# Global contexts in 96-row chunks, the global pieces of a step beside its local contexts, score copies on ScalarE

## The chip, the core and the metric

The kernel runs on one core of a Trainium2 chip. The metric is the device time of one execution in microseconds. In this text PE is TensorE (matmuls and transposes), ACT is ScalarE, DVE is VectorE, POOL is GpSimd, and SP starts the DMAs. "mm" is one matmul instruction.

## What is computed

The reference is a windowed attention with 32 global positions, followed by two feed-forward blocks, all in float32:

```python
s_g = scale * q_g @ k_all.T                      # global queries see everything
out_g = sm(s_g) @ v_all
s_ll = where(|i - j| <= 32, scale * q_l @ k_l.T, -1e9)
s_lg = scale * q_l @ k_g.T
out_l = sm(concat(s_lg, s_ll)) @ concat(v_g, v_l)
x = concat(out_g, out_l)  ->  (2176 tokens used, 512)
h = max(x @ w1, x @ w2, x @ w3);  y = h @ w_out          # 512 -> 768 -> 512
out = softplus(y @ w2_in) @ w2_out                       # 512 -> 2048 -> 512
```

There are 4 batches, 8 heads of width 64, 512 local and 32 global positions. The weights arrive as 64-bit words and are decoded to float32 on the chip.

## The kernel before

**Attention.** The local work is cut into 32 groups `k` (batch, half of the 512 positions, pair of heads). A generator, `att_stream`, runs step `k`: `s1(k)` makes the masked scores of group k in PSUM (matmuls with 64 rows of contraction into 64 columns, the form 64\*64 in the profile) and lets DVE copy them out with their minimum (L154); `s1e` is the exponential on ACT (L161); `s1f` divides by the sum (DVE L167, POOL L171). `s2` transposes group k-2 on PE (L221, L222) and `s2e` copies the two transposed tiles `pwt` and `pgt` out of PSUM. `s3` multiplies group k-3 with the values (L248, L252, form 128\*64) and `s3h`, `s3l` copy the result out as a high and a low part.

**Global queries.** In every odd step `s1g` makes a part of the global scores (L187, L193, form 128\*64). After the fourth pair of a half, `gsoft` does their softmax, `g2` transposes them (L287, L290), `g2e` copies them into the tile `gt`, and in the next step `g3` multiplies them with the values: five chunks of 128, 128, 128, 64 and 96 rows, two heads each, for two pairs of heads (L311, 20 mm, which the trace shows as 40), and `g3e` copies that out.

**Feed forward, first block.** `up(u, f, i)` is one product set: 12 mm of 128\*128 for unit u (256 or 288 tokens), column block f and weight i (L540 to L542). `rest` takes the maximum of the three (ACT L551, DVE L554). `split_h` splits it into a high part `hh` (copy on ACT for u = 0, 1, 7 and on DVE otherwise, L569, L571) and a low part `hl` (L572). `down` is the product with `w_out` (L586 to L588). `dec_stream` decodes the 24 weights of the first block, four DVE instructions, two on ACT and one on POOL each.

**What sets the order.** Every engine runs its instructions in the order in which the program issues them. The program interleaves by counters: `step()` advances the attention by one `yield`, `more(x)` by x of them on average, and `fill`, `part(x)` advance the decoding. Steps below `KS` = 12 run first, with few product sets between them. Then all sets of units 0 and 1 follow with `FJ` = 2.3 yields of decoding each; from then on 1.35 (`RA`) attention yields follow each product set and 1.4 (`RD`) or 1.35 each down block. PSUM tiles of attention and products come from one pool, `pm`, of five buffers (`ptile`).

In steps from 12 on, the global pieces stand behind the fourth `yield` of the step, so product sets lie between them and the local pieces:

```python
for c in late:
    g3(*c)
if k < n and k % 2 == 1:
    s1g(k)
for c in late:
    g3e(*c)
```

The second block (lines from 1063 on) follows after the attention and is not touched.

Of the kernel before, what the change touches and what calls it, by code (L numbers as in the profile page):

```python
# [21 lines left out]
def body(ctx, tc, kq, vw, vb, qg, w1, w2, w3, w_out, w2_in, w2_out, out):  # L22
# [6 lines left out]
    KS = 12  # L29
    HHA = 2  # L30
    HLP = 6
    XLP = 0
    wp = ctx.enter_context(tc.tile_pool(name="wp", bufs=24, side="left"))
# [167 lines left out]
    def gsoft():  # L201
        t = gpend.pop(0)
        nm = at.tile([128, 1], F32, tag="gnm", name="gnm")
        sm = at.tile([128, 1], F32, tag="gsm", name="gsm")
        nc.vector.tensor_reduce(out=nm, in_=t, axis=mybir.AxisListType.X, op=ALU.min)
        yield 0
        nc.scalar.activation(t, t, AF.Exp, scale=-1.0, bias=nm, accum_out=sm)
        yield 0
        nc.vector.tensor_scalar(sm, sm, 1e-9, None, op0=ALU.add)
        nc.vector.reciprocal(sm, sm)  # L210
        nc.vector.tensor_scalar(t, t, sm, None, op0=ALU.mult)
        yield 0
# [12 lines left out]
    def s2e(k):  # L225
        g = st[k]
        pw, pg = g.pop("p")
        if k < KW:
            pwt = wp.tile([128, 512], F32, tag="w", name="pwt")
        else:  # L230
            pwt = at.tile([128, 512], F32, tag="pwt", name="pwt", bufs=1)
        pgt = at.tile([128, 128], F32, tag="pgt", name="pgt", bufs=3)
        nc.scalar.activation(pgt, pg, AF.Copy)  # L233
        if k >= KS or k % 2 == 0:
            nc.scalar.activation(pwt, pw, AF.Copy)
        else:
            nc.vector.tensor_copy(pwt, pw)
        g["pgt"], g["pwt"] = pgt, pwt
# [34 lines left out]
    def s3l(k):  # L273
        b, hf, pr = groups[k]
        po = st.pop(k)["po"].rearrange("p u n -> p (u n)")
        if (2 * b + hf, pr) in direct:
            xh, xl = xs[2 * b + hf]
            nc.vector.tensor_tensor(xl[:, pr:pr + 1, 0:256], po.unsqueeze(1), xh[:, pr:pr + 1, 0:256].bitcast(F32), op=ALU.subtract)

    def g2(b, s):  # L280
        c = gs[b, s]
        t = c["t"]
        chunks = [(0, 128), (128, 128), (256, 128), (384, 64), (448, 96)]
        pa = ptile([128, 512], "pa")
        pb = ptile([128, 128], "pb")
        gt = at.tile([128, 5, 128], F32, tag="gt", name="gt", bufs=1)
        nc.tensor.transpose(pb[0:96], t[:, 448:544], ident)  # L287
        for i in range(4):
            o, n = chunks[i]
            nc.tensor.transpose(pa[0:n, 128 * i:128 * i + 128], t[:, o:o + n], ident)  # L290
        c["gt"], c["p"] = gt, (pa, pb)
# [8 lines left out]
    def g3(b, s, joint=None):  # L300
        c = gs[b, s]
        gt, v0, v1 = c["gt"], c["v0"]["v"], c["v1"]["v"]
        vs = [(v0, 0, 128), (v0, 2, 128), (v1, 0, 128), (v1, 2, 64), (v1, 3, 96)]
        if joint is None:
            joint = ptile([128, 64], "pog")
        po = joint.rearrange("p (a n) -> p a n", n=32)
        for e in range(2):
            for j, (v, u, n) in enumerate(vs):
                for i in range(2):
                    h = 2 * e + i  # L310
                    nc.tensor.matmul(po[64 * i:64 * i + 64, e, :], lhsT=v[0:n, u, 64 * h:64 * h + 64], rhs=gt[0:n, j, 32 * h:32 * h + 32],  # L311
                                     start=(j == 0), stop=(j == 4), skip_group_check=True)
        c["po"] = po
# [11 lines left out]
    def att_stream():  # L325
        n = len(groups)
        load_kq(0)
        load_kq(1)
# [11 lines left out]
        yield 0  # L340
        late = []
        soft = iter(())
        p2 = p3 = um = ng = 0
        for k in range(n + 4):
# [4 lines left out]
            if k < KS:  # L349
# [12 lines left out]
                for c in late:  # L362
                    g3(*c, None if joint is None else joint[:, 288:352])
                if gq and q3 is not None:
                    s3h(q3)
                if gq and q2 is not None:
                    s2e(q2)
                s1e(k, 0)
                s1e(k, 1)
                if not (gq) and q3 is not None:  # L370
                    s3h(q3)
                if k:
                    s1f(k - 1)
                next(soft, None)
                if not (gq) and q2 is not None:
                    s2e(q2)
# [12 lines left out]
                for c in late:  # L389
                    g3e(*c)  # L390
                    ng += 1
                late = []
                if gq:
# [3 lines left out]
            else:  # L397
                if k == KS:
                    s1f(k - 1)
                if k < n:  # L400
                    s1(k, 0)
                    s1(k, 1)
                e3, e2 = (k - 3, k - 2) if k < n else (k - 2, n - 1)
                while p3 < p2 and p3 <= e3 or p2 <= e2:
                    if p3 < p2 and p3 <= e3:
                        s3(p3)
                        s3h(p3)
                        s3l(p3)
                        p3 += 1
                    if p2 <= e2:  # L410
                        s2(p2)
                        s2e(p2)
                        p2 += 1
# [6 lines left out]
                if k < n:  # L420
                    s1f(k)
                for c in late:
                    g3(*c)
                if k < n and k % 2 == 1:
                    s1g(k)
                for c in late:
                    g3e(*c)
                    ng += 1
                late = []
                next(soft, None)  # L430
# [131 lines left out]
    def split_h(u, f):  # L562
# [4 lines left out]
        m = ms.pop((u, f))  # L567
        if HHA > u or u == 7:
            nc.scalar.activation(hh, m, AF.Copy)  # L569
        else:  # L570
            nc.vector.tensor_copy(hh, m)  # L571
        (nc.gpsimd if u == 0 and f < HLP else nc.vector).tensor_tensor(hl, m, hh.bitcast(F32), op=ALU.subtract)  # L572

    def down(u, c, by_row=False):
# [3 lines left out]
        for f0, f1 in [(f, f + 1) for f in range(6)] if by_row else ((0, 5), (5, 6)):  # L578
            for j in range(2):
                p = ps[j]  # L580
                cs = slice(128 * (c + j), 128 * (c + j) + 128)
                for f in range(f0, f1):
# [4 lines left out]
                    nc.tensor.matmul(p, lhsT=w[:, 0, cs], rhs=hl, start=False, stop=False)  # L587
                    nc.tensor.matmul(p, lhsT=w[:, 1, cs], rhs=hh, start=False, stop=(f == 5))  # L588
        for j in range(2):
            o = hp.tile([128, 288], F32, tag="m", name="o")[:, 0:n]  # L590
# [234 lines left out]
    with tc.manual_schedule():  # L825
# [3 lines left out]
        cp = sp = pe = None  # L829
        FJ = 2.3  # L830
        AD = 3
# [3 lines left out]
        NS = 1  # L835
        D2L = 3.0
        D3L = 2.0
# [15 lines left out]
        RJ = 0.7  # L853
        RD = 1.4
        RA = 1.35
        au = [0]
# [8 lines left out]
        def more(x):  # L865
            nx[0] += x
            while nx[0] >= 1:
                nx[0] -= 1
                step()
# [24 lines left out]

        lag[0] = 3
        next(att)
# [14 lines left out]
        flush()  # L911
        lag[0] = 2
        while pos[1] < 18:
# [9 lines left out]
        for _ in range(AD):  # L923
            step()
            part(1.5)
        lag[0] = 0
# [27 lines left out]
        for u in range(6):  # L954
# [11 lines left out]
            for v, f, i in pairs_of(u):  # L966
                up(v, f, i)
                more(RA)
                wide(VU)
# [12 lines left out]
            for c in range(4):  # L982
# [4 lines left out]
                if u == 0:  # L987
                    fill(FD)
                more(RD if u < 2 else RA)
                wide(VD0)  # L990
                spill(SD)
            for _ in ldx:
                pass
            if u == 0:
                for f in range(6):
                    if f >= 1:
                        for _ in range(0):
                            step()
                    split_h(1, f)
                for _ in range(AS):  # L1000
                    step()
# [437 lines left out]
```

## Time and profile before

| | |
|---|---|
| time, median of 3 runs | 768.58 us (768.45 to 768.88) |
| profiled execution, its own time | 769.23 us |
| span of the profile | 767.5 us |
| PE busy | 749.8 us, 98% |
| DVE, ACT, POOL busy | 568.9, 371.9, 252.5 us |
| granted TensorE clock | 1.00 |

"Busy" is the time in which at least one instruction of an engine runs. Matmuls overlap in the pipeline, so on PE the distance from one start to the next says what an instruction costs, not its duration.

### The profile page before, as it was taken

To read this page: it belongs to the slowest core of one execution; us is meant where nothing else is said; L and a number is where in the kernel's file an instruction comes from. 1 tells how busy PE (TensorE), PEld (TensorE's weight loads), DVE (VectorE), ACT (ScalarE), POOL (GpSimd) and SP (SyncE) were. 2 spreads that over 40 slices of the span, in tenths; PEclk is the share of its full clock that TensorE was granted. 3 is DMA by queue.
4 is the path that set the end of the run, shared out by engine and by line. 5 is a ranking of instruction groups with operands and counts; after the bars stand their busy time and mean duration, and the time that the engine had idled before them with its cause. 6 is when DMAs were issued, how large, how long until landed. Compare 5 with 4: busy or idle time off the path is not lost.

```text
span 767.5 us, 18081 instructions
## 1 busy us (share of the span) xinstructions
PE 749.8 (98%) x6984; PEld 722.0 (94%) x6984; DVE 568.9 (74%) x1435; ACT 371.9 (48%) x950; POOL 252.5 (33%) x243
## 2 busy tenths in 40 slices
PE   6899999999999999999999999999999999999998
PEld 4689998999999999999999999999999999999998
DVE  6999956878776777785971656444686889999996
ACT  6875537655544643343322555434554344444443
POOL 4545532122111100443840688842981000000000
PEclk9999999999999999999999999999999999999999
DMA  9858107775867745776101554435549913444432
GB/s 338 317 205 327 41 38 239 238 257 200 278 206 233 239 139 193 275 256 220 43 1 56 184 197 142 175 144 179 183 151 387 374 49 111 138 137 138 139 97 83
DMA packets 78182, 141.03 MB, mean 184 GB/s; under 512 B 9360, under 2 KB 43280, under 8 KB 78096
## 3 DMA queue, kind: packets, MB, share of 16 engines
q1 hardware_dynamic: 78096, 139.88, 53.0%
q8 instruction: 55, 0.90, 0.5%
q14 instruction: 31, 0.25, 0.1%
HBM read 95.03 MB, written 44.83 MB: 182 GB/s over the span
## 4 chain that ended last, share of the span: by engine, by line
PE 77%; DVE 10%; ACT 4%; issue 3%; POOL 3%; DMA 2%; SPq 1%; DVEq 0%; POOLq 0%; ACTq 0%
PE pu L540 8%; PE pu L542 8%; PE pu L541 8%; PE z L1244 6%; PE z L1068 6%; PE z L1069 6%; PE z L1067 6%; PE z L1243 6%; PE z L1242 6%; PE ps L148 2%; PE pd L587 2%; PE pw L221 2%; PE po L248 2%; PE pd L588 2%; PE pd L586 2%
## 5 line engine op out<-in xcount | busy, mean ns | idle before, releaser
L540 PE MATMUL pu<-xh,w 128*128 128x256 f32 (+1 forms) x576 | 168.7, 293 | 0.4 <-ACT pgt L233 0.4
L541 PE MATMUL pu<-xl,w 128*128 128x256 f32 (+1 forms) x576 | 166.3, 289 | 0.0
L542 PE MATMUL pu<-xh,w 128*128 128x256 f32 (+1 forms) x576 | 166.0, 288 | 0.2 <-POOL w L477 0.2
L1244 PE MATMUL z<-v,oo 128*128 128x256 f32 x480 | 136.8, 285 | 0.5 <-DVE oo L1238 0.5
L1243 PE MATMUL z<-v,oo 128*128 128x256 f32 x480 | 135.5, 282 | 0.0
L1242 PE MATMUL z<-v,oo 128*128 128x256 f32 x480 | 135.2, 282 | 0.0
L1068 PE MATMUL z<-o,wi 128*128 128x272 f32 x448 | 129.1, 288 | 1.6 <-POOL o L673 1.6
L1069 PE MATMUL z<-o,wi 128*128 128x272 f32 x448 | 129.1, 288 | 0.0
L1067 PE MATMUL z<-o,wi 128*128 128x272 f32 x448 | 128.7, 287 | 0.1
L540 PEld LDWEIGHTS pu<-xh,w 128*128 128x128 f32 x576 | 108.7, 189 | 2.8 <-issue 1.2
L542 PEld LDWEIGHTS pu<-xh,w 128*128 128x128 f32 x576 | 108.3, 188 | 0.4 <-POOL w L477 0.4
L541 PEld LDWEIGHTS pu<-xl,w 128*128 128x128 f32 x576 | 108.6, 189 | 0.0
L1237 ACT ACTIVATE oo<-sm 128x640 fp32r<-128x640 f32 (+1 forms) x72 | 49.8, 692 | 93.7 <-DVE sm L1232 87.8
L1244 PEld LDWEIGHTS z<-v,oo 128*128 128x128 f32 x480 | 90.9, 189 | 1.4 <-DVE oo L1238 0.9
L1242 PEld LDWEIGHTS z<-v,oo 128*128 128x128 f32 x480 | 91.2, 190 | 0.1
L1243 PEld LDWEIGHTS z<-v,oo 128*128 128x128 f32 x480 | 90.9, 189 | 0.0
L1068 PEld LDWEIGHTS z<-o,wi 128*128 128x128 f32 x448 | 84.2, 188 | 2.3 <-POOL o L673 2.2
L171 POOL TENSOR_TENSOR s<-s,rs 128x512 f32<-128x512 f32 x32 | 35.3, 1103 | 151.0 <-DVE rs L168 85.0
L1067 PEld LDWEIGHTS z<-o,wi 128*128 128x128 f32 x448 | 84.5, 189 | 0.3 <-DVE h L1089 0.3
L1069 PEld LDWEIGHTS z<-o,wi 128*128 128x128 f32 x448 | 84.2, 188 | 0.0
L1238 DVE TENSOR_TENSOR oo<-sm,oo 128x640 fp32r<-128x640 f32 (+1 forms) x72 | 55.1, 765 | 16.5 <-ACT oo L1237 12.8
L673 POOL TENSOR_TENSOR o<-ot,o 128x544 fp32r<-128x544 f32 x36 | 50.9, 1426 | 45.8 <-DMA ot<-od 33.8
(165 smaller groups left out, 1642.1 us busy)
## 6 DMA issues: line engine op xcount, KB each, us to landing
gd<-a SPq DMA_DIRECT2D x32, 544.0 KB, 3.2
gl<-gd SPq DMA_DIRECT2D x32, 512.0 KB, 7.1
kq<-in_kq_dram SPq DMA_DIRECT2D x31, 368.0 KB, 5.1
raw<-in_w_out_dram SPq DMA_DIRECT2D x22, 512.0 KB, 4.5
raw<-in_w_dram SPq DMA_DIRECT2D x18, 512.0 KB, 6.5
vt<-in_vw_dram SPq DMA_DIRECT2D x16, 512.0 KB, 5.9
raw<-in_w_in_dram SPq DMA_DIRECT2D x16, 512.0 KB, 4.4
ot<-od SPq DMA_DIRECT2D x24, 272.0 KB, 3.2
```

Source lines behind the costliest of these rows:

```text
L540: nc.tensor.matmul(p, lhsT=w[:, 0, k], rhs=xh[:, k, 0:n], start=(k == 0), stop=False)
L541: nc.tensor.matmul(p, lhsT=w[:, 0, k], rhs=xl[:, k, 0:n], start=False, stop=False)
L542: nc.tensor.matmul(p, lhsT=w[:, 1, k], rhs=xh[:, k, 0:n], start=False, stop=(k == 3))
L673: nc.gpsimd.tensor_tensor(w[:, 1], src, w[:, 0].bitcast(F32), op=ALU.subtract)
L1067: nc.tensor.matmul(z, lhsT=w[:, 0, k], rhs=x[:, 0, k], start=st and k == 0, stop=False, skip_group_check=True)
L1068: nc.tensor.matmul(z, lhsT=w[:, 0, k], rhs=x[:, 1, k], start=False, stop=False, skip_group_check=True)
L1069: nc.tensor.matmul(z, lhsT=w[:, 1, k], rhs=x[:, 0, k], start=False, stop=sp and k == 1, skip_group_check=True)
L1237: nc.scalar.activation(oh[:, a:b], src, AF.Copy)
L1238: nc.vector.tensor_tensor(ol[:, a:b], src, oh[:, a:b].bitcast(F32), op=ALU.subtract)
L1242: nc.tensor.matmul(p, lhsT=oh[:, a], rhs=w[:, 0], start=st, stop=False, skip_group_check=True)
L1243: nc.tensor.matmul(p, lhsT=oh[:, a], rhs=w[:, 1], start=False, stop=False, skip_group_check=True)
L1244: nc.tensor.matmul(p, lhsT=ol[:, a], rhs=w[:, 0], start=False, stop=sp, skip_group_check=True)
```

## The change

Five things change; the amount of arithmetic on PE stays the same, instruction for instruction.

1. `gt` is allocated once, its rows 64 to 95 of chunk 3 are set to zero once, and the fourth chunk of `g3` contracts 96 rows instead of 64 (the added rows are zero on one side).
2. In steps from 12 on, `s1g`, `g3` and `g3e` are issued by `globals_of(k)` right behind `s3`, `s3h`, `s3l` of the step, `s1g` ahead of `g3`.
3. `pwt` is always copied by ACT (before: by DVE in odd steps below 12).
4. `hh` of unit 2 is copied by ACT.
5. The counters change: `FJ` 2.3 to 2.1, `D2L` (decoding yields per early step) 3.0 to 2.5; attention yields per product set 1.35, 1.35, 1.1, 1.3 for units 2 to 5; per down block 1.8 for unit 0, 1.3 for unit 1 and 1.4 beyond.

All other new names are off (0) and issue nothing.

```diff
-    HHA = 2
+    HHA = 3
...
-        if k >= KS or k % 2 == 0:
+        if not PWD >> k & 1:
             nc.scalar.activation(pwt, pw, AF.Copy)
         else:
             nc.vector.tensor_copy(pwt, pw)
...
-        gt = at.tile([128, 5, 128], F32, tag="gt", name="gt", bufs=1)
+        gt = gts[0]
...
-        vs = [(v0, 0, 128), (v0, 2, 128), (v1, 0, 128), (v1, 2, 64), (v1, 3, 96)]
+        vs = [(v0, 0, 128), (v0, 2, 128), (v1, 0, 128), (v1, 2, 96), (v1, 3, 96)]
...
+        gts.append(at.tile([128, 5, 128], F32, tag="gt", name="gt", bufs=1))
+        nc.vector.memset(gts[0][64:96, 3, :], 0.0)
...
+        def globals_of(k):
+            nonlocal ng
+            if todo[0] is None:
+                return
+            todo[0] = None
+            odd = k < n and k % 2 == 1
+            joint = ptile([128, 352], "psg") if JN and (late or odd) else None
+            if odd:
+                s1g(k, None if joint is None else joint[:, 0:288])
+            for c in late:
+                g3(*c, None if joint is None else joint[:, 288:352])
+            for c in late:
+                g3e(*c)
+                ng += 1
+            late.clear()
...
                         s3h(p3)
                         s3l(p3)
                         p3 += 1
+                        if ORD:
+                            globals_of(k)
...
-                for c in late:
-                    g3(*c)
-                if k < n and k % 2 == 1:
-                    s1g(k)
-                for c in late:
-                    g3e(*c)
-                    ng += 1
-                late = []
+                globals_of(k)
...
-        FJ = 2.3
+        FJ = 2.1
...
-        D2L = 3.0
+        D2L = 2.5
...
-        RD = 1.4
-        RA = 1.35
+        RD = 1.8
+        RA2 = 1.35
+        RA3 = 1.35
+        RA4 = 1.1
+        RA5 = 1.3
+        RD1 = 1.3
+        RE = 1.4
```

**PE, step 21.** Before, in PE's queue, the local pieces and the global scores of step 21 (`ps` scores, `po` contexts, `pw` and `pg` transposes, `psg` global scores, `pu` products):

```order
L542 MATMUL pu<-xh,w 128x256
L148 MATMUL ps<-kq 64x160 x8
L248 MATMUL po<-pgt,vb 64x2x64 x4
L252 MATMUL po<-pwt,vt 64x64 x8
L221 MATMUL pw<-ident,s 128x128 x4
L222 MATMUL pg<-ident,sg 128x128
L540 MATMUL pu<-xh,w 128x256
...
L542 MATMUL pu<-xh,w 128x256
L187 MATMUL psg<-kq,qg 64x256 x2
L193 MATMUL psg<-kq,qg 64x32 x2
L540 MATMUL pu<-xh,w 128x256
```

With the change (the same pieces under their new line numbers):

```order
L578 MATMUL pu<-xh,w 128x256
L164 MATMUL ps<-kq 64x160 x8
L267 MATMUL po<-pgt,vb 64x2x64 x4
L271 MATMUL po<-pwt,vt 64x64 x8
L203 MATMUL psg<-kq,qg 64x256 x2
L209 MATMUL psg<-kq,qg 64x32 x2
L240 MATMUL pw<-ident,s 128x128 x4
L241 MATMUL pg<-ident,sg 128x128
L576 MATMUL pu<-xh,w 128x256
```

The global scores no longer stand between two product sets. Of the 12 places from step 12 on where `s1g`, `g3` or both stood by themselves, 11 move like this; the last one, behind the last group, stays by itself.

**ACT, step 3.** Before, in ACT's queue, from the exponentials of step 3 (`s`) to those of step 4:

```order
L161 ACTIVATE s,sm<-s,nm 128x160 x4
L267 ACTIVATE xh<-po 128x256
L233 ACTIVATE pgt<-pg 128x128
L190 ACTIVATE gsc<-psg 128x256
L476 ACTIVATE w<-tmp 128x512
L161 ACTIVATE s,sm<-s,nm 128x160 x4
```

With the change:

```order
L177 ACTIVATE s,sm<-s,nm 128x160 x4
L286 ACTIVATE xh<-po 128x256
L252 ACTIVATE pgt<-pg 128x128
L254 ACTIVATE pwt<-pw 128x512
L206 ACTIVATE gsc<-psg 128x256
L512 ACTIVATE w<-tmp 128x512
L177 ACTIVATE s,sm<-s,nm 128x160 x4
```

One `pwt` copy has come in; on DVE one has gone from the same step. The same happens in steps 5, 7, 9, 11 and 13.

**ACT, the split of unit 1.** Before, in ACT's queue, around the six `hh` copies for which the down products of unit 1 wait (`tmp` is the decoding of the second block, `gsc` the global softmax):

```order
L633 ACTIVATE tmp<-raw 128x512
L161 ACTIVATE s,sm<-s,nm 128x160 x4
L207 ACTIVATE gsc,gsm<-gsc,gnm 128x544
L569 ACTIVATE hh<-m 128x288 x6
L267 ACTIVATE xh<-po 128x256
```

With the change:

```order
L673 ACTIVATE tmp<-raw 128x512
L177 ACTIVATE s,sm<-s,nm 128x160 x2
L605 ACTIVATE hh<-m 128x288 x6
L177 ACTIVATE s,sm<-s,nm 128x160 x2
L223 ACTIVATE gsc,gsm<-gsc,gnm 128x544
```

Two of the four exponentials and the softmax have moved behind the copies.

## Rows read from the trace of the kernel before

**Rows 1.** The page: the span, and the busy time of each engine.

```profile
span 767.5 us, 18081 instructions
PE 749.8 (98%) x6984; PEld 722.0 (94%) x6984; DVE 568.9 (74%) x1435; ACT 371.9 (48%) x950; POOL 252.5 (33%) x243
```

**Rows 2.** Windows: stretch, its length, busy us (instructions) by engine, clock, DMA.

```profile
0.00:33.00 33.00, 23.16 (x303) 16.76 (x303) 24.43 (x101) 24.41 (x86) 16.70 (x31) 1.00 0.92 342
33.00:101.00 68.00, 67.60 (x688) 63.78 (x686) 65.43 (x162) 41.32 (x116) 36.94 (x35) 1.00 0.52 191
101.00:127.00 26.00, 24.60 (x299) 21.66 (x298) 11.98 (x48) 13.89 (x48) 5.44 (x7) 1.00 0.41 128
127.00:304.00 177.00, 176.63 (x2028) 164.44 (x2027) 132.96 (x416) 92.51 (x294) 31.29 (x36) 1.00 0.66 221
304.00:768.00 464.00, 457.83 (x3675) 455.33 (x3673) 334.08 (x712) 199.80 (x410) 162.16 (x134) 1.00 0.47 160
```

**Rows 3.** Waits of PE: what waited, for whom, us in total, times, longest.

```profile
PE po L248 <- ACT pgt L233: 2.8, 4, 1.0
PE pd L586 <- ACT hh L569: 0.9, 1, 0.9
```

**Rows 4.** Timeline of PE, one g3, in narrow windows: start, us, form, merged count.

```profile
145.78 1.84 PE L311 MATMUL pog<-gt,vt 128*64 128x32 f32 x40
146.63 0.40 PE L311 MATMUL pog<-gt,vt 128*64 128x32 f32 x8
146.86 0.29 PE L311 MATMUL pog<-gt,vt 128*64 128x32 f32 x4
147.08 0.25 PE L311 MATMUL pog<-gt,vt 64*64 64x32 f32 x2
147.31 0.30 PE L311 MATMUL pog<-gt,vt 96*64 96x32 f32 x3
147.45 0.41 PE L187 MATMUL psg<-kq,qg 128*64 128x256 f32 x2
```

**Rows 5.** Timeline of PE: a product set behind step 12; step 21 and its global scores.

```profile
104.00 0.40 PE L540 MATMUL pu<-xh,w 128*128 128x288 f32 x1 [0.37 <-ACT pgt L233]
...
174.02 0.79 PE L148 MATMUL ps<-kq 64*64 64x160 f32 x16
...
175.63 0.23 PE L252 MATMUL po<-pwt,vt 128*64 128x64 f32 x2
175.79 0.33 PE L221 MATMUL pw<-ident,s 128*128 128x128 f32 x1
...
179.01 0.28 PE L541 MATMUL pu<-xl,w 128*128 128x256 f32 x1
179.13 0.28 PE L542 MATMUL pu<-xh,w 128*128 128x256 f32 x1
179.34 0.44 PE L187 MATMUL psg<-kq,qg 128*64 128x256 f32 x2
```

**Rows 6.** Groups by line and form: the two copies of pwt; busy, mean ns.

```profile
L235 ACT ACTIVATE pwt<-pw 128x512 f32<-128x512 f32 x26 | 15.4, 593 | 0.0
L237 DVE COPY pwt<-pw 128x512 f32<-128x512 f32 x6 | 4.0, 675 | 0.4 <-PE pw L221 0.4
```

**Rows 7.** Timeline of ACT: first exponentials of steps 4 and 6, idle time before.

```profile
20.10 0.43 ACT L161 ACTIVATE s<-s,nm 128x160 f32<-128x160 f32 x1 [0.93 <-DVE nm L154]
28.24 0.43 ACT L161 ACTIVATE s<-s,nm 128x160 f32<-128x160 f32 x1 [0.20 <-DVE nm L154]
```

**Rows 8.** Timeline of ACT ahead of the down products of unit 1.

```profile
124.71 0.74 ACT L207 ACTIVATE gsc<-gsc,gnm 128x544 f32<-128x544 f32 x1
...
125.44 2.10 ACT L569 ACTIVATE hh<-m 128x288 fp32r<-128x288 f32 x6
```

**Rows 9.** Timeline of PE and DVE: transposes of a g2, and the last copy into gt.

```profile
206.03 0.49 PE L290 MATMUL pa<-ident,gsc 128*128 128x128 f32 x3
...
209.33 0.27 DVE L298 COPY gt<-pa 64x128 f32<-64x128 f32 x1
```

More of the change, by code (lines that the diff above doesn't have):

```diff
@@ L29, in body @@
     KS = 12
-    HHA = 2
+    HHA = 3
     HLP = 6
+    E2 = 0
+    E3 = 0
+    ORD = 1
+    GM = 0
+    HS0 = 0
+    HS1 = 0
+    HS2 = 0
+    HS3 = 0
+    HE = 0x3F
+    HP = 0
+    JN = 0
+    PWD = 0
+    LA = 3
+    LB = 2
+    PA = 1.5
+    SM = 1
     XLP = 0
@@ L210, in gsoft @@
         nc.vector.reciprocal(sm, sm)
-        nc.vector.tensor_scalar(t, t, sm, None, op0=ALU.mult)
+        if GM:
+            nc.scalar.activation(t, t, AF.Copy, scale=sm)
+        else:
+            nc.vector.tensor_scalar(t, t, sm, None, op0=ALU.mult)
         yield 0
@@ L278, in s3l @@
             nc.vector.tensor_tensor(xl[:, pr:pr + 1, 0:256], po.unsqueeze(1), xh[:, pr:pr + 1, 0:256].bitcast(F32), op=ALU.subtract)
+    gts = []
     def g2(b, s):
@@ L340, in att_stream @@
         yield 0
-        late = []
+        late, todo = [], [None]
         soft = iter(())
+        def globals_of(k):
[13 more added lines that the diff above has]
+            late.clear()
         p2 = p3 = um = ng = 0
@@ L363, in att_stream @@
                     g3(*c, None if joint is None else joint[:, 288:352])
-                if gq and q3 is not None:
+                if (gq or k >= E3 > 0) and q3 is not None:
                     s3h(q3)
-                if gq and q2 is not None:
+                if (gq or k >= E2 > 0) and q2 is not None:
                     s2e(q2)
@@ L369, in att_stream @@
                 s1e(k, 1)
-                if not (gq) and q3 is not None:
+                if not (gq or k >= E3 > 0) and q3 is not None:
                     s3h(q3)
@@ L374, in att_stream @@
                 next(soft, None)
-                if not (gq) and q2 is not None:
+                if not (gq or k >= E2 > 0) and q2 is not None:
                     s2e(q2)
@@ L391, in att_stream @@
                     ng += 1
-                late = []
+                late.clear()
                 if gq:
@@ L399, in att_stream @@
                     s1f(k - 1)
+                todo[0] = k
                 if k < n:
@@ L421, in att_stream @@
                     s1f(k)
-                for c in late:
-                    g3(*c)
-                if k < n and k % 2 == 1:
-                    s1g(k)
-                for c in late:
-                    g3e(*c)
-                    ng += 1
-                late = []
+                globals_of(k)
                 next(soft, None)
@@ L567, in split_h @@
         m = ms.pop((u, f))
-        if HHA > u or u == 7:
+        if (HHA > u and (u != 1 or HE >> f & 1)) or u == 7:
             nc.scalar.activation(hh, m, AF.Copy)
+        elif u == 1 and HP >> f & 1:
+            nc.gpsimd.tensor_copy(hh, m)
         else:
@@ L588, in down @@
                     nc.tensor.matmul(p, lhsT=w[:, 1, cs], rhs=hh, start=False, stop=(f == 5))
+            if by_row and f0 < HS0:
+                split_h(1, f0)
         for j in range(2):
@@ L893, in ready @@
             return pos[u] < 18 and pos[u] < len(W) - (MG if len(W) < 24 else 0)
-        lag[0] = 3
+        lag[0] = LA
         next(att)
@@ L911, in body @@
         flush()
-        lag[0] = 2
+        lag[0] = LB
         while pos[1] < 18:
@@ L924, in body @@
             step()
-            part(1.5)
+            part(PA)
         lag[0] = 0
@@ L967, in body @@
                 up(v, f, i)
-                more(RA)
+                more((RA2, RA3, RA4, RA5)[v - 2])
                 wide(VU)
@@ L988, in body @@
                     fill(FD)
-                more(RD if u < 2 else RA)
+                if u == 0 and c == 2:
+                    for f in range(HS0, HS1):
+                        split_h(1, f)
+                more(RD if u == 0 else RD1 if u == 1 else RE)
                 wide(VD0)
                 spill(SD)
+                if u == 0 and c >= 2:
+                    for f in range(max(HS0, HS1), HS2) if c == 2 else range(HS2, HS3):
+                        split_h(1, f)
             for _ in ldx:
@@ L994, in body @@
             if u == 0:
[L995 to L998, printed above, removed]
+                for f in range(max(HS0, HS1, HS2, HS3), 6):
                     split_h(1, f)
```

## The prediction

> **What bounds the kernel now.** I read the page first: PE is busy for 749.8 of 767.5 us and no other engine for more than 74% of the span [rows 1]. Then the table by stage, to see where PE's missing 17.7 us are: 9.84 us before 33 us, 0.4 us from 33 to 101, 1.4 us from 101 to 127, 0.4 us from 127 to 304, and some 6 us in the rest, which holds the end and the second block [rows 2]. So in nearly all of the program PE is never idle, and an instruction that costs PE less time shortens the run by as much, as long as PE stays without waits. In the first 33 us DVE is busy for 24.4 us and ACT for 24.4 us; from 33 to 101 us DVE is busy for 65.4 of 68 us, nearly as full as PE [rows 2]. Then the list of PE's waits: the long ones in the part that the change touches are for copies on ACT [rows 3].
>
> Because a busy PE is not a cheap one, I looked at distances between starts. They show what a change of form costs. In a g3, four pairs of 128\*64 mm take from 146.63 to 146.86, 0.058 us each pair; the 64-row chunk, two pairs, takes from 147.08 to 147.31, 0.23 us, and the 96-row chunk behind it 0.14 us; and the third chunk of 128 rows, which ends in the change to 64 rows, takes 0.22 us instead of 0.117 [rows 4]. Leaving the form 128\*64 for the 128\*128 of a transpose costs 0.16 us from the last pair, and entering it from a product costs 0.21 us, where products follow each other every 0.12 us [rows 5].
>
> **The change part by part.** The sum is made against the profiled execution's own 769.23 us; it stands 0.65 us above the median of 768.58 us, and the prediction is given on the median.
>
> *96 rows.* A g3 now takes from 145.78 to 147.45, 1.67 us [rows 4]. Behind a 96-row chunk the next 128-row chunk follows without a gap (0.14 us for that chunk, of which 0.02 us is a slower first step, and 0.23 us for the next four pairs), so I take 96 rows to belong to the same form as 128. Then 20 pairs cost 20 x 0.058 = 1.17 us and an entry of 0.02 us: 0.48 us less, for eight of them 3.8 us. The trace doesn't show a step from 128 to 96 rows. If that cost what the step from 128 to 64 does (0.22 - 0.12 = 0.10 us), each half of a g3 would shrink from 0.82 us (146.63 to 147.45) to 0.35 + 0.10 + 0.14 + 0.12 = 0.71 us, in all 1.8 us. I take 3.8, since the nearest row is the step from 96 to 128. The zeroing is one small DVE instruction ahead of the first scores, while DVE has nothing: nothing, and 0.3 us (the length of a similar copy, the last of rows 9) if it has.
>
> The Trainium skill's page "TensorEngine Tiling (Array Packing)", section "Key Properties", says that a change of the tiling mode drains TensorE, and lists modes of 128, 64 and 32 rows only. By it a step from 128 to 96 rows is no change of mode; the row on 96 to 128 agrees, and the sum would be the same 3.8 us.
>
> *Global pieces behind the local contexts.* Before, the contexts leave their form (0.16 us to the transposes), and later the global pieces enter it from a product (0.21 us) and leave it again. After, they follow in the same form, by a pair step of 0.06 us, leave it once, to the transposes, and the two products that stood around them follow each other at 0.12 us [rows 5]. That is 0.16 + 0.21 - 0.06 - 0.12 = 0.19 us each, for 11 places 2.1 us. The step from local to global pieces is not in the trace; between nothing and a full entry of 0.21 us it gives 2.8 to 0.4 us. I take 2.1, because the pairs within the form are the nearest row.
>
> What it moves: `g3` now comes earlier behind the copies into `gt`. In one g2 the last of these ended at 209.60, some 3.2 us behind the transposes, which end near 206.4 [rows 9]. The new distance is a product set (12 x 0.12 = 1.4 us), the scores and contexts (174.02 to 175.79, 1.8 us) and the global scores (at least 0.4 us) [rows 5]: 3.6 us, just enough. In one step of unit 3 the order puts no product set between: 2.2 us, so up to 1.0 us of waiting. Also, five PSUM tiles are now taken in a row in odd steps. A product set waited for such a tile's copy for 0.37 us at 104 us [rows 5]. I allow 0.9 us for both, with bounds of nothing and 1.9 us.
>
> *pwt to ACT.* One copy costs 0.675 us on DVE and 0.593 us on ACT [rows 6]. In the first 33 us two steps, 3 and 5, carry it. ACT then stands idle for 0.93 us ahead of the exponentials of step 4 and 0.20 us ahead of those of step 6, both times for DVE [rows 7]. So in step 3 the copy fits, and the following scores come some 0.6 us sooner; in step 5 ACT becomes the later engine, and gives 0.2 to 0.4 us back. I take a gain of 0.4 us; bounds are 1.3 us (both copies in full) and a loss of 0.4 us (0.59 - 0.20, nothing won on DVE). In 33 to 101 us the four other copies relieve DVE, the fuller engine: PE, without waits there, gains nothing, but the decoding gets 2 to 3 us of reserve.
>
> *Counters.* The same 24 weights are decoded, with fewer yields per set, and units 0 and 1 alternate more strictly; DVE gets its reserve from the copies, so I expect no wait for weights. Step 12 now starts behind the last product set of unit 1. The wait of 0.37 us at 104 us stood where a set followed that step, with the maxima of two earlier sets outstanding [rows 5]; now they are done first: -0.4 us. The split of unit 1 cost PE 0.9 us [rows 3]. Ahead of its `hh` copies, the softmax (124.71 to 125.44, 0.73 us) and two exponentials (0.4 us each) move behind them [rows 7, 8]; that covers the wait, but the `hl` on DVE come next: I take -0.7 us, with bounds of nothing and -1.0 us. The DMAs of groups shift by a place in SP's queue against the writes of results; they are issued four steps ahead.
>
> *hh of unit 2.* Six ACT copies, 2.10 / 6 = 0.35 us each in a row [rows 8], replace six on DVE, in a stage with ACT at 92.5 and DVE at 133.0 of 177 us [rows 2]: nothing; without that cover, one copy, 0.35 us, ahead of the last down products.
>
> Sum: -3.8 - 2.1 - 0.4 - 0.4 - 0.7 + 0.9 = -6.5 us. From 769.23 that is 762.7, and on the median 768.58 - 6.5 = **762.1 us**.
>
> **The rivals.**
>
> *A, the other side: PE waits for PSUM in the joined steps.* In each of the 10 odd steps from 13 on, the copy of the global scores now stands on ACT ahead of `pgt` and `pwt`, and the next product needs one of the five tiles. If each waited as long as the down products waited for ACT, 0.9 us [rows 3], that costs 9.0 us against the 7.4 us won above: 768.6 + 1.6 = 770.2 us. It decides against the change from 0.74 us per step. For it speaks that PE has waited for just this; against it, ACT is busy for only 52% of that stage and PE waited for 0.4 us in all of it [rows 2].
>
> *B: the form costs stay.* The step to 96 rows costs 0.10 us and the first joined piece a full entry: 1.8 + 0.4 instead of 5.9 us, 765.8 us. That is the change not doing what it says. Against it stands the step from 96 to 128 rows.
>
> *C: ACT binds the start.* The copies land on the path in full (a loss of 0.4 instead of a gain), and the `hh` copies of unit 1 wait as before: 762.1 + 0.8 + 0.7 = 763.6 us. For it: ACT is as busy as DVE in the first 33 us.
>
> *D: fewer rows were the better form.* If 64 rows let two chunks run side by side, widening the 16 chunks would lose half a pair step for each of their 32 pairs, 32 x 0.03 = 0.9 us, instead of winning 3.8: 766.8 us. The rows speak against it: a 64-row chunk takes 0.23 us, twice a 128-row one [rows 4]. The Trainium skill's page "TensorEngine Tiling (Array Packing)", section "When to Use Tiling", advises row tiling for a contraction of 64 or fewer, for up to twice the speed; by that rule the change would lose, and the 64-row chunks of this trace don't show it.
>
> **How the numbers follow.** Chances: the forecast 0.73, A 0.06, B 0.10, C 0.08, D 0.03. The bounds of the single terms put the forecast's own range at 759.6 to 765.0 us: down by the larger joining (0.7), start (0.9) and no new wait (0.9), up by 1.0 more of waiting, half of the joining (1.0) and of the 96-row term (0.9). To leave out no more than 2 in 10, the range has to take in C and B: 759.5 to 766.5 us; A, D and the rest of the tail stay outside. A measurement of this kernel can tell about 0.2% (1.5 us) from no change, so faster means below 767.0 us: the forecast, B, C and most of D, 0.91 with some of the forecast's tail given away; within 0.2% 0.05; slower 0.04, nearly all of it A.
>
> **What the profile after would show.** A g3 of about 1.2 us from its first start to the next piece; 96\*64 mm in the place of 64\*64; `psg` behind `po` with a first step near 0.06 us; PE idle for about 0.4 us less before 33 us, with the exponentials of step 6 waiting for ACT itself rather than DVE; no wait at the products behind step 12, and one of 0.2 to 0.3 us, for `hl`, at the first down product of unit 1. The prediction fails if new waits for `gt`, for PSUM tiles or for weights of units 0 and 1 add up to more than 2 us between 33 and 304 us, or if a 96-row chunk shows its own entry cost.

## The result and the profile after

The changed kernel takes 760.42 us (median of 4 runs, 760.23 to 761.05) against 768.73 us for the kernel before beside it (4 runs, 768.45 to 769.05): ratio 0.9891, 95% interval 0.9876 to 0.9907, 8.3 us less. The forecast was 762.1 us, the range 759.5 to 766.5. The page of the profiled execution (760.23 us by its own time), span and busy times, against [rows 1]:

```profile
span 758.5 us, 18066 instructions
PE 740.2 (98%) x6984; PEld 717.2 (95%) x6984; DVE 566.8 (75%) x1424; ACT 377.3 (50%) x962; POOL 251.3 (33%) x243
```

PE has the same 6984 instructions and is busy for 9.6 us less; the span is 9.0 us shorter. (That is more than the 8.3 us of the medians, because the profiled execution before, 769.23 us, lies 0.5 us above its median and the one after 0.2 us below.) The work of PE has become cheaper, and its idle time is about the same: 18.3 us against 17.7 us. The windows of the profile after, against [rows 2] (the last two bounded 9 us earlier, where the same work ends):

```profile
0.00:33.00 33.00, 22.06 (x305) 15.68 (x306) 25.41 (x104) 25.55 (x90) 16.82 (x31) 1.00 0.90 341
33.00:101.00 68.00, 68.00 (x702) 64.97 (x701) 64.82 (x157) 43.58 (x118) 36.82 (x35) 1.00 0.48 178
101.00:127.00 26.00, 24.29 (x304) 22.04 (x303) 13.37 (x53) 15.27 (x53) 6.73 (x9) 1.00 0.52 182
127.00:295.00 168.00, 167.63 (x1974) 158.81 (x1973) 127.92 (x397) 92.29 (x292) 28.93 (x35) 1.00 0.69 229
295.00:759.00 464.00, 458.17 (x3707) 455.74 (x3705) 335.30 (x717) 200.61 (x413) 162.00 (x134) 1.00 0.47 160
```

PE is idle for 10.9 us before 33 us (9.8 before), not at all from 33 to 101 us (0.4), 1.7 us from 101 to 127 (1.4), 0.4 us in the stage behind it (0.4). Where the 9.0 us come from is seen from four points of PE's timeline, before and after: the first product set starts at 32.94 and 32.53 us (-0.4), the first of unit 2 at 138.89 and 135.98 (-2.9), the first of unit 6 at 345.88 and 336.91 (-9.0), the second block at 418.66 and 409.69 (-9.0). Two thirds are won between 139 and 346 us, where PE hardly waited before or after.

The waits of PE after, against [rows 3]:

```profile
PE po L267 <- ACT pgt L252: 4.4, 6, 1.1
PE ps L164 <- issue: 1.3, 1, 1.3
PE pd L625 <- DVE hl L610: 0.4, 1, 0.4
```

The first stands in the first 33 us for the most part (4.1 us, 2.4 before). The second and the third are new at their places; both belong to the split of unit 1, and together they are longer than the 0.9 us that stood there before.

One g3 after, in PE's timeline, from the global scores ahead of it to the transposes behind, and the groups of `g3` by form (busy, mean ns):

```profile
139.24 0.60 PE L203 MATMUL psg<-kq,qg 128*64 128x256 f32 x4
139.67 1.31 PE L332 MATMUL pog<-gt,vt 128*64 128x32 f32 x40
140.91 0.66 PE L240 MATMUL pw<-ident,s 128*128 128x128 f32 x4
...
L332 PE MATMUL pog<-gt,vt 128*64 128x32 f32 x144 | 6.1, 221 | 0.0
L332 PE MATMUL pog<-gt,vt 96*64 96x32 f32 x96 | 4.9, 223 | 0.0
```

From its first start to the next piece a g3 takes 1.24 us, where it took 1.67 us [rows 4]; 96\*64 stands in the place of 64\*64. The two are not quite alike: before, the next piece had the form of g3, and now it is a transpose, so that leaving the form is in the 1.24 us. Experiment 1 has both with the same piece behind.

Step 21 after, in PE's timeline (the contexts end, the global scores follow, then the transposes), and what stood behind the global scores of the same step before:

```profile
171.18 0.23 PE L271 MATMUL po<-pwt,vt 128*64 128x64 f32 x2
171.24 0.39 PE L203 MATMUL psg<-kq,qg 128*64 128x256 f32 x2
...
171.67 0.26 PE L209 MATMUL psg<-kq,qg 128*64 128x32 f32 x4
171.86 0.33 PE L240 MATMUL pw<-ident,s 128*128 128x128 f32 x1
```

```profile
179.82 0.26 PE L193 MATMUL psg<-kq,qg 128*64 128x32 f32 x4
180.00 0.39 PE L540 MATMUL pu<-xh,w 128*128 128x256 f32 x1
180.23 0.28 PE L541 MATMUL pu<-xl,w 128*128 128x256 f32 x1
```

The first global scores follow the contexts by 0.06 us, without an entry cost. What the joining is worth in this step can be read off. Before, from the last product ahead of the scores (179.13, [rows 5]) to the second product behind them (180.23) it was 1.10 us; without the scores it would be two steps of 0.12 us, so they cost 0.86 us. After, from the last pair of contexts to the transposes it is 0.68 us; without the scores it was 0.16 us, so they cost 0.52 us. The difference is 0.34 us, where I had reckoned 0.19 us.

### The profile page after: what moved, and what is told of

Read it like the earlier page. It is cut to its first block, busy times and chain, and to the rows that moved or that the text cites. A ratio compares the mean times of both kernels' runs of the same rounds, so it can differ in the third digit from the quotient of the medians.

```text
span 758.5 us, 18066 instructions
## 1 busy us (share of the span) xinstructions
PE 740.2 (98%) x6984; PEld 717.2 (95%) x6984; DVE 566.8 (75%) x1424; ACT 377.3 (50%) x962; POOL 251.3 (33%) x243
## 4 chain that ended last, share of the span: by engine, by line
PE 83%; DVE 5%; DMA 4%; ACT 3%; POOL 3%; issue 2%; SPq 0%; ACTq 0%; DVEq 0%; POOLq 0%
PE pu L576 10%; PE pu L577 10%; PE pu L578 10%; PE z L1292 6%; PE z L1291 6%; PE z L1290 6%; PE z L1116 6%; PE z L1117 6%; PE z L1115 6%; PE pd L625 2%; PE pd L626 2%; PE pd L624 2%; PE ps L164 2%; PE po L267 2%; PE pw L240 2%
## 5 line engine op out<-in xcount | busy, mean ns | idle before, releaser
L1168 ACT ACTIVATE a<-h 128x816 f32<-128x816 f32 x32 | 28.4, 887 | 76.3 <-DVE h L1146 76.3
```

## The experiments

**1. 96 rows alone.** The kernel before, with this and the zeroed `gt` only:

```diff
-        vs = [(v0, 0, 128), (v0, 2, 128), (v1, 0, 128), (v1, 2, 64), (v1, 3, 96)]
+        vs = [(v0, 0, 128), (v0, 2, 128), (v1, 0, 128), (v1, 2, 96), (v1, 3, 96)]
```

> The kernel before with the 96-row chunk and the zeroed tile alone. Theory of the form (a change between 64*64 and 128*64 costs some 0.1 us to go in and 0.1 us to come out, 96 rows are no change): each g3 takes about 1.2 instead of 1.67 us, 3.8 us less in all, with bounds of 1.8 and 3.9 us. Rival (64 rows are the cheaper form): 0 to 0.9 us more. Rival (PE is not what sets the time, the gain is lost in waits behind): g3 shorter, but the total less than 2 us lower.

Measured: 765.27 us, ratio 0.9956 (0.9944 to 0.9969), 3.4 us less, with 2.4 to 4.3 us inside the interval. In PE's timeline of this run the g3 of [rows 4], with the same global scores behind it:

```profile
145.17 1.36 PE L313 MATMUL pog<-gt,vt 128*64 128x32 f32 x40
146.36 0.63 PE L187 MATMUL psg<-kq,qg 128*64 128x256 f32 x4
```

That is 1.19 us instead of 1.67, and each of the eight g3 is shorter by the same 0.48 us: 3.8 us, just the predicted term, and within what the times can tell.

**2. The same 64-row chunks, put beside each other.** The kernel before; the second pair of heads of a g3 begins with its 64-row chunk, where the first pair ends with it:

```diff
-            for j, (v, u, n) in enumerate(vs):
+            js = (0, 1, 2, 4, 3) if e == 0 else (3, 4, 0, 1, 2)
+            for j in js:
+                v, u, n = vs[j]
...
-                                     start=(j == 0), stop=(j == 4), skip_group_check=True)
+                                     start=(j == js[0]), stop=(j == js[-1]), skip_group_check=True)
```

> The kernel before, chunks of 64 rows kept, but the 64-row chunks of the two pairs of heads of a g3 made neighbours: the same matmuls, half as many changes of form. Theory of the form change: about half of what the 96-row chunk brings, 1.9 us less (0.24 us for each of the eight g3). Rival (the 64-row matmuls themselves are slow, twice a 128-row pair): no change, within 0.3 us.

Measured: 766.68 us, 0.9979 (0.9970 to 0.9988), 2.0 us less. The matmuls are the same in another order, only 16 of the 32 changes into or out of the 64-row form are gone: 0.12 us each (each g3 takes 1.43 us instead of 1.67). So it is the change of form that costs, not the rows; all 32 would be 3.9 us, near the 3.8 us that the 96 rows take off the eight g3.

**3. Joining alone.** The kernel before with `globals_of(k)` behind `s3l`:

```diff
+                        globals_of(k)
...
-                for c in late:
-                    g3(*c)
-                if k < n and k % 2 == 1:
-                    s1g(k)
...
+                globals_of(k)
```

> The kernel before with the global pieces behind the local contexts alone. By the prediction's term: 0.19 us for each of 11 places, 2.1 us less. By the theory after the result, that the second instruction of a product set behind a foreign form is late too (0.23 instead of 0.12 us, which the sum left out): 0.30 us each, 3.3 us less. Rival A (ACT's longer queue in the joined steps makes PE wait for PSUM): less than 1 us gained, with waits of PE for ACT at the products behind odd steps.

Measured: 766.93 us, 0.9980 (0.9971 to 0.9989), only 1.7 us less. I summed, in each trace, the distances from one start to the next of all PE instructions from the first product set on, without the idle time; called PE's steps below. (A part of each wait is in the steps: idle time counts from the modelled end of the instruction before, so a step that ends in a wait is 0.07 to 0.27 us longer than the same step without one.) Here the steps are 3.3 us shorter than before, but PE idles 1.7 us more. ACT's and then PE's timeline of this run:

```profile
120.20 0.68 ACT L643 ACTIVATE tmp<-raw 128x512 f32<-128x512 f32 x1 [3.91 <-DMA raw<-in_w_in_dram]
...
122.88 0.79 PE L148 MATMUL ps<-kq 64*64 64x160 f32 x16 [1.94 <-issue]
...
265.75 0.39 PE L550 MATMUL pu<-xh,w 128*128 128x256 f32 x1 [0.64 <-DVE m L564]
```

ACT stands at the first decoding of `w2_in` for its words, and the scores of step 15 come 1.94 us late; later a product waits 0.64 us for the maximum of an earlier set, which frees its PSUM tile.

**4. pwt on ACT alone.** The kernel before:

```diff
-        if k >= KS or k % 2 == 0:
-            nc.scalar.activation(pwt, pw, AF.Copy)
-        else:
-            nc.vector.tensor_copy(pwt, pw)
+        nc.scalar.activation(pwt, pw, AF.Copy)
```

> The kernel before with all pwt copies on ACT alone. Theory: DVE sets the pace of the first steps, the first product set starts about 0.4 us sooner, and PE waits less for weights and maxima at 43 and 61 us (0.4 us there): 0.4 to 0.8 us less in all. Rival C (ACT binds the start): no change or up to 0.4 us more, with the exponentials of step 6 no longer waiting for DVE.

Measured: 768.69 us against 768.62, 1.0002 (0.9994 to 1.0011): nothing.

**5. The counters alone** (`FJ`, `D2L`, `RD`, `RD1`, `RE` and the `RA`s of the diff, in the kernel before):

> The kernel before with the new counters alone. By the prediction: the wait behind step 12 and the wait at the split of unit 1 go, 1.1 us less. By the theory after the result: the first goes (0.4 us less), but ACT's wait for the first weights of the second block now lies ahead of the exponentials of step 13 and PE waits at the scores of step 15 for 1.0 to 1.5 us instead of 0.9 us at the split: within 0.5 us of before.

Measured: 768.62 us, 1.0001 (0.9992 to 1.0010): nothing. In the trace the waits at 43, 61 and 104 us are gone (0.21, 0.19 and 0.37 us before), but from 118 to 126 us PE waits for 0.54, 0.83 (the scores of step 15) and 0.96 us (`hl`), where it waited for 1.03 us before.

**6. All but the counters** (96 rows, joining, `pwt`, `hh`; the counters of before):

> The kernel before with all instruction changes (96 rows, joined global pieces, pwt and hh of unit 2 on ACT) and the old counters. If the terms add up: 3.8 + 3.3 + 0.6 = 7.7 us less than before. If the counters are needed for it (the freed DVE time is only used with them): at least 1.5 us worse than the changed kernel.

Measured: 763.19 us, 0.9927 (0.9915 to 0.9940). That is 5.4 us less than before, about as much as the single edits together (3.4 + 1.7 + 0 us), and 2.8 us more than the full change. PE idles 1.1 us more than in the full change, and its steps are 1.4 us longer; of these, 1.1 us are in steps that end in a wait, so most of the difference is waits. Three of them in PE's timeline; the kernel after has none in the place of the first two, and 1.27 us in the place of the third:

```profile
61.35 0.39 PE L553 MATMUL pu<-xh,w 128*128 128x256 f32 x1 [0.85 <-POOL w L488]
...
103.97 0.40 PE L551 MATMUL pu<-xh,w 128*128 128x288 f32 x1 [0.37 <-ACT pgt L233]
...
122.25 0.39 PE L148 MATMUL ps<-kq 64*64 64x160 f32 x4 [0.84 <-PE pg L222]
```

**7. The full change with the pieces apart again:**

```diff
-    ORD = 1
+    ORD = 0
```

> The kernel after with the global pieces again behind the fourth yield of a step (global scores still ahead of global contexts). Theory (joining worth 3.0 to 4.5 us by changes of form and late second products): 763.5 to 765.0 us. Rival (0.19 us for each of 11 places as predicted, and nothing else moves): 762.5 us. Second rival: with the new counters the pieces stand beside each other anyway: within 0.7 us of 760.4.

Measured: 764.63 us (763.86 to 764.88), 0.9945 (0.9930 to 0.9960). So joining is worth 4.2 us here. PE's steps are 3.4 us longer than after (0.4 us of it in steps that end in a wait), its idle time is 0.5 us longer: with these counters, joining costs no new wait on balance.

**8. One counter back.** The full change with the old number of attention yields per down block of unit 0:

```diff
-        RD = 1.8
+        RD = 1.4
```

> The changed kernel with 1.4 instead of 1.8 attention yields per down block of unit 0. Theory that the faster steps put the exponentials of step 13 behind ACT's read wait: with 1.4 yields the step stands later against the read, PE's wait of 1.27 us at the scores of step 15 is gone, and something like the 0.9 us at the split of unit 1 comes back: within 0.6 us of the changed kernel. Rival (the wait does not hang on this counter): the 1.27 us stay.

Measured: 765.62 us (763.88 to 767.13), 0.9961 (0.9947 to 0.9975). My expectation was wrong by 5 us, and the wait that was to go, at the scores of step 15, is longer (2.04 us). Its PE timeline (the transposes of a g2 at 299.72, then its g3):

```profile
121.06 0.79 PE L164 MATMUL ps<-kq 64*64 64x160 f32 x16 [2.04 <-issue]
...
143.32 1.36 PE L332 MATMUL pog<-gt,vt 128*64 128x32 f32 x40 [0.76 <-DVE m L590]
...
299.72 0.60 PE L311 MATMUL pa<-ident,gsc 128*128 128x128 f32 x4
300.96 0.54 PE L332 MATMUL pog<-gt,vt 128*64 128x32 f32 x12 [0.64 <-ACT gt L318]
301.98 1.01 PE L332 MATMUL pog<-gt,vt 96*64 96x32 f32 x28 [0.47 <-DVE gt L319]
...
377.01 0.40 PE L576 MATMUL pu<-xh,w 128*128 128x288 f32 x1 [0.42 <-DVE m L590]
```

Waits of the two kinds that the prediction allowed for are here, though not all at its places. A g3 stands right behind the transposes of its g2, without a product set between, and waits 0.64 and 0.47 us for the copies into `gt`. It is the last g3, which isn't joined: four down blocks give 0.4 yields less each, the g2 doesn't come before the end of unit 4's down blocks any more, and the program issues what is left of the attention in one go ahead of unit 5. A joined g3 (143.32) and two products (266.94, 0.27 us, and 377.01) wait for the maxima of product sets, which free PSUM tiles; why the last of these, behind the attention, waits is open. In all, PE idles 3.5 us more than after, and its steps are 1.5 us longer, 1.2 us of it in steps that end in a wait.

The five g3 that are joined start 0.33 to 1.25 us behind the last copy into `gt` in the kernel after, where the same five had 3.70 to 5.29 us before. So joining has used up most of that reserve, but in no run does a joined g3 wait for `gt`; in this one the closest starts as the last copy ends.

**9. hh of unit 2 on DVE again** (`HHA` 3 to 2 in the kernel after):

> The kernel after with the hh copies of unit 2 on DVE as before. Theory, as predicted: nothing is late on either engine there, 760.4 us within 0.5 us. Rival: DVE is needed for the global softmax and the transposes' copies of that stage, and PE waits for it: 761.2 us or more, with a wait of PE between 180 and 195 us.

Measured: 760.86 us (760.75 to 761.09), 0.9898 (0.9881 to 0.9915), and no wait of PE between 180 and 195 us: nothing that can be told apart, as predicted.

**10. The words of w2_in read early.** What made the scores of step 15 late after? The timelines of ACT, DVE and PE in the kernel after:

```profile
115.92 0.77 ACT L673 ACTIVATE tmp<-raw 128x512 f32<-128x512 f32 x1 [3.27 <-DMA raw<-in_w_in_dram]
...
118.42 0.17 DVE L183 TENSOR_SCALAR rs<-sm 128x4 f32<-128x4 f32 x1 [0.81 <-ACT s L177]
...
118.72 0.29 DVE L170 CUSTOM_DVE_ANT_0 s<-ps,mask 128x160 f32<-128x160 f32 x1
...
119.86 0.79 PE L164 MATMUL ps<-kq 64*64 64x160 f32 x16 [1.27 <-issue]
...
123.49 0.40 PE L625 MATMUL pd<-hl,w 128*128 128x288 f32 x1 [0.44 <-DVE hl L610]
```

The chain is to be read from the top: ACT waits 3.27 us for a DMA, so the exponentials of step 13 behind it are late; DVE waits for them ahead of the copies of the scores of step 14; these copies empty the only `ps` tile, which the scores of step 15 need. The page calls the last wait "issue". In the kernel after:

```diff
         dv, d4, lo0 = words(), iter(()), iter(())
+        fill(99)
+        next(dv)
```

> The changed kernel with the first two reads of the second block's weights issued ahead of the down products of unit 0 instead of behind their first results. Theory: in the changed kernel ACT waits 3.3 us for that read ahead of the exponentials of step 13, DVE waits for these, the scores of step 14 are copied late, and PE waits 1.27 us at the scores of step 15 and 0.44 us at the first down products of unit 1; without the late read both go, 1.0 to 1.7 us less, 759.0 us. Rival (the wait is the decoding work on ACT and DVE itself, or the counters' order): PE still waits there, less than 0.4 us gained.

Measured: 760.01 us (759.64 to 760.27), 0.9888 (0.9874 to 0.9901). The 1.27 us are gone with the late read, which shows the chain from its first to its last link, but PE's timeline has another wait next, and ACT's shows what it waits for:

```profile
123.97 0.42 ACT L212 ACTIVATE gsc<-psg 128x288 f32<-128x288 f32 x1
...
124.44 0.40 PE L624 MATMUL pd<-hh,w 128*128 128x288 f32 x1 [0.98 <-ACT gsc L212]
```

**11. That copy on DVE as well.** The next down product starts when the copy of the global scores ends, and their PSUM tile comes free:

```diff
-            nc.scalar.activation(t[:, 256:544], ps, AF.Copy, scale=-scale)
+            if k == 15:
+                nc.vector.tensor_scalar(t[:, 256:544], ps, -scale, None, op0=ALU.mult)
+            else:
+                nc.scalar.activation(t[:, 256:544], ps, AF.Copy, scale=-scale)
```

> The kernel after with the first words of w2_in read early (760.0 us, PE waits 0.98 us at 124.44 for a down product of unit 1), and the copy of the global scores of step 15 (L212) on DVE instead of ACT. Theory: that product waits for the PSUM tile of these global scores, whose copy stands on ACT behind six hh copies, two exponentials and the global softmax; on DVE it follows the hl instructions, which end at 123.1, so PE starts some 0.7 us sooner: 759.3 us. Rival: it waits for hh or for ACT otherwise, no change: 760.0 us within 0.3 us.

Measured: 759.49 us (758.97 to 759.71), 0.9879 (0.9864 to 0.9894). It is the lowest median of all, but neither it nor experiment 10 can be told from the kernel after: the intervals overlap. In the trace my theory holds only by half:

```profile
124.48 0.28 ACT L255 ACTIVATE pgt<-pg 128x128 f32<-128x128 f32 x1
...
124.82 0.40 PE L627 MATMUL pd<-hh,w 128*128 128x288 f32 x1 [0.83 <-ACT pgt L255]
```

The wait did go to the next tile in ACT's queue, `pg`, and shrank by 0.15 us instead of 0.7. Behind six `hh` copies ACT has every PSUM tile of this place in its queue.

**12. Joining alone, with the words read early** (experiments 3 and 10 in one):

> The kernel before with the joined pieces alone, and the first words of w2_in read before the steps from 12 on begin. Theory formed after the run of the joined pieces alone: joining takes about 4.5 us off the distances between PE's starts, more than twice the 2.1 us predicted, and 1.9 us of that were lost at the scores of step 15, which came late behind the read of those words. Then the early read gives most of it back: 765.0 to 765.6 us, with no wait over 0.3 us of PE for the scores of step 15. Rival 1: joining is worth 1.7 us and the wait at step 15 only stands in for another one at the split of unit 1: 766.5 to 767.2 us, with a new wait of about 1 us there.

Measured: 766.03 us (765.55 to 766.47), 0.9966 (0.9953 to 0.9979), between the two expectations. The scores of step 15 come in time, but ahead of the `hh` copies there is now a wait of 1.11 us (125.32 us), with the softmax and a `tmp` of the decoding in front of them in ACT's queue. PE's steps are 3.5 us shorter than before, as in experiment 3.

The runs beside each other, times in us; PE's steps and idle time are those from the first product set on, in the profiled execution:

| kernel | median | steps | idle |
|---|---|---|---|
| before | 768.6 | 726.5 | 4.7 |
| 1, 96 rows | 765.27 | 722.6 | 4.8 |
| 3, joining | 766.93 | 723.2 | 6.4 |
| 12, joining, early words | 766.03 | 723.0 | 4.9 |
| 5, counters | 768.62 | 725.3 | 4.9 |
| 6, all but the counters | 763.19 | 719.7 | 5.4 |
| 7, all but the joining | 764.63 | 721.7 | 4.8 |
| 8, `RD` 1.4 | 765.62 | 719.8 | 7.8 |
| after | 760.42 | 718.3 | 4.3 |
| 11, early words and copy | 759.49 | 718.5 | 3.5 |

## Why the prediction was right, and where its terms were not

**What bounds the kernel** held: PE's instructions got cheaper (busy for 9.6 us less), PE waited little more in all (0.6 us: 1.1 us more before 33 us, less behind), and the span got shorter by 9.0 us.

**96 rows, -3.8 us:** right. Alone it measured -3.4 us in the time, with 3.8 inside the interval, and 8 x 0.48 = 3.8 us in the g3 themselves (experiment 1). The step from 128 to 96 rows costs nothing, as the row on 96 to 128 had it. The page "TensorEngine Tiling (Array Packing)" of the Trainium skill, section "Key Properties", says that a change of the tiling mode drains TensorE; experiments 1 and 2 agree, with 0.12 us for a change between 64 and 128 rows.

**Joining, -2.1 us:** the mechanism was right, the term mis-sized. It is 4.2 us in the full change (experiment 7), 3.3 to 3.5 us of them in PE's steps (experiments 3, 7 and 12). The step that failed is "0.16 + 0.21 - 0.06 - 0.12 = 0.19 us each": it counts the late first instruction of an entry and leaves out what is late behind it. The second product behind a foreign form came 0.23 instead of 0.12 us after the first (180.00 to 180.23), and the four global scores took 0.48 us behind a product (179.34 to 179.82) and 0.43 behind the contexts (171.24 to 171.67): 0.11 + 0.05 us more, 0.35 us in this step. The steps of the runs, without what waits add to them, give 0.27 us (experiment 7) and 0.32 us (experiment 3) a place on the mean; waits make most of the rest of the 4.2 us.

**New waits, +0.9 us:** none of those named is in the kernel after. With one counter changed (experiment 8) a joined g3 and products waited for PSUM tiles, as allowed for; a g3 waited for `gt` too, but the last one, which isn't joined.

**Counters, -0.4 and -0.7 us:** the wait behind step 12 went, as predicted. The split of unit 1 did not win 0.7 us; the stretch has 1.71 us of waits instead of 1.03 us (0.94 and 0.09), from a chain that I hadn't looked for, the words of `w2_in`. Alone the counters are worth nothing in the time (experiment 5): they take 0.8 us of waits away before 105 us and add 1.3 us around the split (PE's steps are 1.2 us shorter in that profile, of which the time shows nothing). Beside the rest they are worth 2.8 us (experiment 6). With the old ones joining wins 1.7 us (experiment 3), with the new ones 4.2 us, though it shortens PE's steps by about as much each time: with the old counters half of that goes into waits (experiment 3: 1.9 us at the scores of step 15, 0.6 us later). I had costed the counters on their own, as a sum of waits. Which of them does what was tried only for `RD`; the traces say in addition that the waits at 43 and 61 us stand in every kernel with the old counters and in none with the new ones.

**pwt to ACT, -0.4 us:** nothing alone (experiment 4), so the term failed: "the following scores come some 0.6 us sooner". The exponentials of step 6 don't wait for DVE any more, as predicted, but the first product set starts at 32.98 us (32.94 before). In that trace PE waits 1.4 us less for `pg` at the scores, 1.0 us more for `pgt` at the contexts and 1.4 us more for the load of `qg`; since that load comes at another time in each execution, how much of the gain ACT takes back stays open. The first product set does start 0.4 us earlier in the kernel after, but that is no evidence: in experiments 8 and 10, which issue the same up to there, it starts at 32.97 and 32.02 us.

**The rivals.** A is refuted for the kernel after: no product there waits for one of the five tiles. Its mechanism exists: in experiments 8, 10 and 11 a down product of unit 1 waits for copies on ACT behind step 15 (0.53, 0.98 and 0.83 us), once, not in each joined step. B and D are refuted by experiments 1, 2 and 7. The advice in "When to Use Tiling" of that page of the Trainium skill, to tile rows for a contraction of 64 or fewer, brought nothing to the 64-row chunks of this kernel: they stood among 128-row ones, and no run here sets two of them on different rows of the array, so the advice itself wasn't tried. C was right that the start wins nothing and that the split still waits, though its loss of 0.4 us at the start isn't seen in experiment 4; the joining made up for both.

So a sum of -6.5 met -8.3 us with errors of both signs, and that it came so near is partly luck: 0.4 (pwt) + 1.4 (split of unit 1: 0.7 us lost instead of won) too hopeful, 2.1 (joining) + 0.9 (waits) too careful. That makes 1.2 of the 1.8 us; the rest, 0.6 us, is within what the times can tell. The two waits at 43 and 61 us (0.4 us in [rows 2]), which the sum put at nothing, went with the counters, and one of 0.26 us for `hl` at 340.33 us is gone too.

What the profile was to show came true for g3 (1.24 us), the form 96\*64, the step of 0.06 us, the exponentials of step 6 (no idle time for DVE before them), the products behind step 12 (no wait) and the `hl` wait (0.44 rather than 0.2 to 0.3 us). PE was not idle for less time before 33 us, but for 1.1 us more.

## What to carry to other kernels

Price a change of form at both ends and one instruction further: measure from the last instruction before the foreign piece to the second behind it. Compare such a piece before and after with the same piece behind it. When pieces are moved together, the counters that set the order become part of the change: an edit that is worth nothing alone decides how much of the other one arrives, and one counter set back can cost more waits far behind its own place than it saves at it. A wait that the page calls "issue" can be followed back through the queues of two engines to a DMA, and removing it may only show the next wait behind the same engine.

## What the runs showed of the hardware that was not expected

Before some 13 to 17 us the same instructions stand further apart. The 16 score mm of a step, in PE's timeline of the kernel after:

```profile
10.56 1.36 PE L164 MATMUL ps<-kq 64*64 64x160 f32 x16
...
13.18 0.79 PE L164 MATMUL ps<-kq 64*64 64x160 f32 x16
```

In the kernel before the group at 13.00 us still took 1.36 us, and the one at 17.76 us 0.79 us. The windows print a granted clock of 1.00 there too, but that is no reading: the trace's record of the clock begins at 12.85 us in the kernel after and at 16.81 us before, with the full clock (2.4 GHz), and a window without a record prints 1.00. In all fourteen traces the groups that end ahead of the first record take 0.89 us or more from the first start to the last, and the next ones behind it 0.49 or 0.50 us. So PE ran slower until then, by the spacing, while it was busy for 6.31 of the 12.85 us (10.43 of 16.81 before); that it was at the lower of its two levels (1.2 GHz) is likely from the ratio of 1.8, but not on record.

When the record begins varies between executions by 4 us (12.85 to 16.81), and so does the arrival of the first loads (PE waited for `qg` for 0.78 us before, 1.51 after, 2.12 in experiment 8). The start of the first product set varies with them, by up to 1 us in kernels that issue the same until then (32.02 to 32.97 us). A single profile can't show a gain of a few tenths there.
